# Class-by-class layout of the filtered spectrum, two tiles' statistics on swapped engines, and a new written-out order

## The chip, the core and the metric

The kernel runs on one NeuronCore of a Trainium2 chip. Five engines work side by side: TensorE (PE) multiplies matrices and writes to PSUM; VectorE (DVE) and ScalarE (ACT) read PSUM and SBUF; GpSimd (POOL) works on SBUF; SyncE (SP) starts most of the DMAs. The metric is the device time of one execution in microseconds, the median of several runs.

## What is computed

The input x has 2048 rows of 640 numbers. Each row is normalized (mean and variance over its 640 numbers). The result is the sum of x and two branches on the normalized rows: a filter in the two-dimensional Fourier domain, and a gated product of three matrices.

```python
def _A_ref(x, w_r, w_i):
    B, S, D = x.shape                                   # 1, 2048, 640
    X = jnp.fft.rfft2(x.astype(jnp.float32), axes=(-2, -1))
    X = X * (w_r + 1j * w_i)                            # (2048, 321)
    return jnp.fft.irfft2(X, s=(S, D), axes=(-2, -1)).astype(jnp.bfloat16)

def _B_ref(x, w_gate, w_up, w_down):                    # 640x1536, 640x1536, 1536x640
    g = jnp.einsum("bsd,df->bsf", x, w_gate)
    u = jnp.einsum("bsd,df->bsf", x, w_up)
    return jnp.einsum("bsf,fd->bsd", g * u, w_down)

x = A_x
xn = _layernorm(x, axis=-1)
return x + _A_ref(xn, A_w_r, A_w_i) + _B_ref(xn, B_w_gate, B_w_up, B_w_down)
```

## The kernel before

The 2048 rows are 16 tiles of 128 (tile b holds rows 16p + b on partition p). The program is a list of tasks, each with an engine, its reads and writes, and PSUM banks. The order of the tasks on every engine and the bank of each are written out by hand in the table `_PLAN` (task number, engine, bank); the semaphore waits follow from it. So an engine takes its tasks strictly in the order of the table, SP's DMAs included. Names below are the task names in the code; a number after an underscore is a tile, a chunk or a frequency group.

**Start.** 42 full matmuls on constants (`warm`) run on PE until the first tile is there; `nwarm` is their number. For each tile the statistics are made either on DVE (`bn`, two halves, then `ag`) or on ACT (`sm` for the mean, `sq` for the sum of squares); the set `aset` says which tiles are on ACT. Then `sd` (square root, ACT), `rs` (reciprocal, DVE) and `mul` (normalize in place, DVE). Tiles 0 to 3 are transposed on PE (`T0_b`, five matmuls, copied out by `eT0_b`), the others by DMA (`xt`). Tile loads are `ld_x`.

**Gate and up.** `GU_f_b_w` multiplies block f of 128 gate or up columns (w) by a chunk of rows that begins with tile b, `eG` copies it to SBUF, and `H_f_b` multiplies gate and up on DVE. This is L973 for small chunks and L951 for chunks of 512 rows.

**Fourier branch, forward.** `S1` to `S5` on DVE and `R` on PE (L905) split the 640 columns by five and two and transform along part of the rows. `D_t_w` (L1034) transforms columns, `eD` copies the result, and `C_t` (L1053) finishes the rows: 321 frequencies for each of 128 combinations, in PSUM. The 321 frequencies come as four classes of 64 (two halves of 32, the second half mirrored) and one class of 65 (every fifth frequency).

**Filter.** `WM_t` on DVE multiplies the result by w_r and w_i, with four instructions for the four classes (L1070, one for each of the two weights and the two halves) and one for the fifth class (L1073). For two t at a time, `SM_t` (L1086, L1087) combines them to real and imaginary parts in the buffer L, and `JA`, `JB` (fifth class: `JC`, `JD`, on POOL) write the parts again with real and imaginary exchanged, so that L holds, for each frequency group q, 640 columns. The weight `ld_w` loads come in pieces.

**Fourier branch, inverse.** `IA_q` (L1116) has five small matmuls, one for each class, whose stationary operand is 128 columns of L and whose moving operand is a table of 64 columns; `eIA` copies to Z2. When all of Z2 is there, `I_a` (L1144) transforms the columns back with the table g, `V1` to `V5` on DVE join the classes to 640 columns, and `IV` (L1233) adds the last step into the PSUM bank of the output.

**Output.** `ACC_a_h` (L1221) multiplies H by w_down for tile a and half h, in three pieces of 5, 4 and 3 matmuls; `IV` ends the group; `FINA` (ACT) and `FIN` (DVE) add x again (loaded once more by `ld_xr`), and `st_out` stores. Blocks of w_down (`ld_wd`) take the place of the inverse row table (`ld_ti`) as it is used up.

In the layout before, the four classes lie interleaved in L, so four of the five stationary operands of an IA are read with a step of 4 elements:

```python
yl = v_l[:, lr, o_ + 128 + k:o_ + 640:4] if k < 4 else v_l[:, lr, o_:o_ + 128]
```

Of the kernel before, what the change touches and what calls it, by code (L numbers as in the profile page):

```python
# [255 lines left out]
def _build_tables():  # L256
    t = {}
# [7 lines left out]
    for tt in range(16):  # L265
        for g in range(_G):
            q = tt * _G + g
# [36 lines left out]
    for o in range(2):  # L304
        own = (l_ % 2 == o).astype(np.float64)
        fd[64 * o:64 * o + 64, 512:577] = e.real * own[None, :]
        fd[64 * o:64 * o + 64, 578:641] = (e.imag * own[None, :])[:, 1:64]
        gd[63:128, 512 + 64 * o:576 + 64 * o] = w.real * own[:, None]
        gd[0:63, 512 + 64 * o:576 + 64 * o] = -(w.imag * own[:, None])[1:64]
# [59 lines left out]
_LP = 321  # L369
_YS = 1090  # L370
# [30 lines left out]
def _d_act(n):  # L401
# [4 lines left out]
    (12, 1, -1), (19, 2, -1), (10, 0, 1), (0, 3, -1), (11, 4, -1), (13, 4, -1), (18, 2, -1), (20, 2, -1), (28, 2, -1),  # L406
    (27, 2, -1), (170, 1, -1), (14, 4, -1), (8, 3, -1), (21, 1, -1), (22, 2, -1), (29, 2, -1), (23, 2, -1), (30, 1, -1),
    (31, 2, -1), (32, 2, -1), (24, 0, 3), (25, 2, -1), (26, 2, -1), (9, 0, 7), (33, 0, 1), (34, 2, -1), (35, 2, -1),
    (181, 0, 0), (182, 2, -1), (36, 1, -1), (37, 1, -1), (15, 4, -1), (43, 1, -1), (38, 1, -1), (169, 4, -1), (179, 0, 6),
    (180, 2, -1), (39, 2, -1), (40, 2, -1), (183, 2, -1), (44, 1, -1), (45, 1, -1), (46, 2, -1), (47, 2, -1), (189, 0, 1),  # L410
    (191, 0, 0), (190, 1, -1), (192, 1, -1), (193, 2, -1), (172, 4, -1), (186, 0, 6), (171, 4, -1), (112, 2, -1), (187, 1, -1),
    (41, 0, 2), (42, 1, -1), (184, 0, 7), (185, 1, -1), (16, 4, -1), (54, 2, -1), (113, 2, -1), (48, 0, 6), (49, 1, -1),
    (62, 1, -1), (194, 0, 5), (196, 0, 3), (197, 1, -1), (195, 1, -1), (188, 2, -1), (198, 2, -1), (50, 2, -1), (51, 2, -1),
    (53, 2, -1), (114, 2, -1), (55, 2, -1), (52, 2, -1), (63, 1, -1), (206, 0, 2), (207, 1, -1), (64, 1, -1), (204, 0, 7),
    (205, 1, -1), (115, 2, -1), (173, 4, -1), (209, 0, 6), (174, 4, -1), (65, 1, -1), (210, 1, -1), (66, 1, -1), (67, 2, -1),
    (56, 1, -1), (57, 2, -1), (116, 2, -1), (199, 0, 3), (200, 1, -1), (70, 2, -1), (201, 0, 2), (202, 1, -1), (203, 2, -1),
    (58, 2, -1), (208, 2, -1), (17, 4, -1), (121, 2, -1), (72, 1, -1), (1, 4, -1), (211, 0, 7), (175, 4, -1), (212, 1, -1),
    (176, 4, -1), (177, 4, -1), (73, 1, -1), (117, 0, 2), (118, 1, -1), (119, 0, 5), (74, 1, -1), (213, 2, -1), (122, 2, -1),
    (68, 2, -1), (123, 2, -1), (75, 1, -1), (76, 1, -1), (77, 2, -1), (216, 0, 1), (217, 1, -1), (214, 0, 0), (215, 1, -1),
    (218, 2, -1), (221, 0, 2), (222, 1, -1), (78, 2, -1), (124, 2, -1), (219, 0, 3), (220, 1, -1), (223, 2, -1), (80, 2, -1),  # L420
    (224, 0, 4), (120, 1, -1), (225, 1, -1), (82, 1, -1), (60, 2, -1), (226, 0, 2), (227, 1, -1), (229, 0, 6), (230, 1, -1),
    (83, 1, -1), (84, 1, -1), (178, 4, -1), (231, 0, 5), (125, 2, -1), (128, 0, 6), (126, 0, 3), (129, 1, -1), (232, 1, -1),
    (228, 2, -1), (130, 2, -1), (233, 2, -1), (131, 2, -1), (59, 4, -1), (71, 4, -1), (2, 4, -1), (236, 0, 0), (237, 1, -1),
    (61, 4, -1), (85, 1, -1), (234, 0, 2), (127, 1, -1), (86, 1, -1), (235, 1, -1), (238, 2, -1), (132, 2, -1), (92, 1, -1),
    (241, 0, 6), (242, 1, -1), (239, 0, 7), (240, 1, -1), (93, 1, -1), (243, 2, -1), (133, 2, -1), (87, 2, -1), (246, 0, 4),
    (244, 0, 1), (245, 1, -1), (94, 1, -1), (247, 1, -1), (248, 2, -1), (134, 2, -1), (69, 4, -1), (249, 0, 6), (250, 1, -1),
    (95, 1, -1), (96, 1, -1), (97, 2, -1), (251, 0, 2), (252, 1, -1), (90, 2, -1), (253, 2, -1), (88, 2, -1), (98, 2, -1),
    (100, 2, -1), (254, 0, 7), (255, 1, -1), (256, 0, 3), (257, 1, -1), (438, 4, -1), (433, 4, -1), (259, 0, 4), (260, 1, -1),
    (258, 2, -1), (137, 0, 5), (139, 0, 0), (437, 4, -1), (435, 4, -1), (441, 4, -1), (472, 4, -1), (101, 4, -1), (91, 4, -1),
    (434, 4, -1), (470, 4, -1), (3, 4, -1), (135, 0, 2), (136, 1, -1), (143, 2, -1), (138, 1, -1), (102, 1, -1), (261, 0, 7),  # L430
    (262, 1, -1), (79, 4, -1), (89, 4, -1), (141, 0, 3), (269, 0, 2), (263, 2, -1), (142, 1, -1), (140, 1, -1), (266, 0, 5),
    (267, 1, -1), (144, 2, -1), (270, 1, -1), (264, 0, 4), (265, 1, -1), (268, 2, -1), (145, 2, -1), (271, 0, 5), (274, 0, 1),
    (103, 1, -1), (104, 1, -1), (272, 1, -1), (273, 2, -1), (81, 4, -1), (442, 4, -1), (466, 4, -1), (146, 2, -1), (105, 1, -1),
    (106, 1, -1), (275, 1, -1), (279, 0, 4), (280, 1, -1), (276, 0, 0), (277, 1, -1), (278, 2, -1), (107, 2, -1), (147, 2, -1),
    (110, 2, -1), (108, 2, -1), (468, 4, -1), (469, 4, -1), (281, 0, 6), (282, 1, -1), (286, 0, 7), (287, 1, -1), (283, 2, -1),
    (284, 0, 3), (152, 0, 4), (148, 0, 6), (153, 1, -1), (99, 4, -1), (431, 4, -1), (440, 4, -1), (432, 4, -1), (4, 4, -1),
    (683, 4, -1), (109, 4, -1), (111, 4, -1), (473, 4, -1), (156, 2, -1), (429, 4, -1), (439, 4, -1), (467, 4, -1), (471, 4, -1),
    (149, 1, -1), (285, 1, -1), (288, 2, -1), (157, 2, -1), (150, 0, 0), (289, 0, 2), (151, 1, -1), (154, 0, 4), (291, 0, 6),
    (296, 0, 0), (290, 1, -1), (292, 1, -1), (155, 1, -1), (293, 2, -1), (158, 2, -1), (301, 0, 2), (299, 0, 6), (300, 1, -1),
    (294, 0, 4), (295, 1, -1), (304, 0, 7), (306, 0, 6), (6, 4, -1), (297, 1, -1), (298, 2, -1), (159, 2, -1), (160, 2, -1),  # L440
    (305, 1, -1), (307, 1, -1), (309, 0, 0), (310, 1, -1), (302, 1, -1), (303, 2, -1), (311, 0, 7), (312, 2, -1), (308, 2, -1),
    (163, 0, 5), (164, 1, -1), (167, 0, 1), (161, 0, 3), (162, 1, -1), (168, 2, -1), (314, 0, 0), (315, 2, -1), (313, 2, -1),
    (165, 0, 4), (316, 0, 6), (317, 2, -1), (166, 1, -1), (446, 0, 2), (447, 1, -1), (448, 2, -1), (474, 0, 0), (443, 0, 4),
# [78 lines left out]
def _build(nc, A_x, A_w_r, A_w_i, B_w_gate, B_w_up, B_w_down, out, opts=None):  # L522
# [3 lines left out]
    with es:  # L526
# [46 lines left out]
        o_end = cur[0]  # L573
        cur[0] = o_r
        b_a = alloc("A", 4 * 648)
        b_pr = alloc("PR", 8 * 321)
        b_l = alloc("L", 2 * 2624)
        b_w3 = alloc("W3", 2 * _WQ * 321)
        o_end = max(o_end, cur[0])
# [14 lines left out]
        def V(name):  # L594
            off, sz = lay[name]
            return arena[:, off: off + sz]
# [748 lines left out]
```

## Time and profile before

| | |
|---|---|
| median of 3 runs (lowest, highest) | 196.58 us (196.56, 196.6) |
| the profiled execution: its time, its span | 196.57 us, 194.9 us |
| granted TensorE clock | 1.00 |
| busy: PE, DVE, ACT, POOL | 190.9, 176.7, 136.4, 12.2 us |
| DVE in the stage 68.3 to 127.2 us | 55.96 of 58.90 us |
| gate and up, 512 rows (L951) | 440 matmuls, 101.9 us busy |
| down (L1221) | 396 matmuls, 57.2 us busy |
| IA (L1116) | 160 matmuls |
| WM (L1070 and L1073) | 64 x 414 ns and 16 x 432 ns |

The span runs from the first to the last instruction of the core; the rest of the execution's time lies around it. In a row of the groups the columns are: line, engine, operation, operands (out<-in) with their shapes, count, then busy time and the mean of one instruction in ns, and last the idle time of the engine just before them with what ended it. Matmuls overlap each other, so the mean of one is longer than the distance from one to the next; the chain gives the time that they take on the path. A piece of the chain gives its start, its length, the engine, the line and the number of instructions.

### The profile page before, as it was taken

The numbers are of one execution on the slowest core, as the hardware profiler recorded it, in microseconds if no ns is written. First come the engines' busy times: TensorE is split into PE (matmuls) and PEld (weight loads), VectorE is DVE, ScalarE is ACT, GpSimd is POOL, SyncE is SP. The second block draws the span as 40 slices with busy tenths as digits, with TensorE's granted clock in tenths as the row PEclk, the third lists the DMA queues.
The fourth block names the chain that finished last, engine by engine and source line by source line (L and its number), as shares of the span: only waits on it lengthen the run. The fifth ranks groups of instructions, "written<-read, shape, count | busy, mean of one in ns | idle before, by whom it ended". The sixth has DMA issues, their size and how long they took to land.

```text
span 194.9 us, 4074 instructions
## 1 busy us (share of the span) xinstructions
PE 190.9 (98%) x1568; PEld 120.5 (62%) x1568; DVE 176.7 (91%) x369; ACT 136.4 (70%) x275; POOL 12.2 (6%) x22
## 2 busy tenths in 40 slices
PE   8899999999999999999999999999999999999995
PEld 8797454454454565555655555557777777777774
DVE  3899999999999999999989999987999999999713
ACT  3899999999884679989999999667305523253130
POOL 1000000000000000331031221120000000000000
DMA  5999974016869921366465510005001543135412
GB/s 173 324 370 324 214 98 111 0 37 105 155 130 222 258 68 27 96 145 193 118 153 135 153 36 31 3 0 170 4 0 53 144 143 104 40 95 172 134 68 67
DMA packets 29666, 23.73 MB, mean 122 GB/s; under 512 B 10448, under 2 KB 27600, under 8 KB 29520
## 3 DMA queue, kind: packets, MB, share of 16 engines
q1 hardware_dynamic: 28848, 23.08, 46.5%
q10 hardware_dynamic: 800, 0.41, 0.7%
q8 instruction: 12, 0.20, 0.5%
q14 instruction: 6, 0.05, 0.1%
HBM read 18.89 MB, written 2.62 MB: 110 GB/s over the span
## 4 chain that ended last, share of the span: by engine, by line
PE 95%; DVE 2%; DMA 1%; ACT 1%; issue 0%
PE ps L951 48%; PE ps L1221 27%; PE ps L973 5%; PE ps L1116 3%; PE ps L1034 2%; PE ps L1053 2%; PE ps L905 2%; PE ps L1144 2%; PE ps L1233 2%; DMA arena<-in_A_x_dram 1%; DVE arena L754 1%; PE ps L814 1%; ACT arena L681 1%; DVE arena L682 0%; DVE arena L761 0%
## 5 line engine op out<-in xcount | busy, mean ns | idle before, releaser
L681 ACT ACTIVATE arena<-ps 128x512 bf16<-128x512 f32 (+5 forms) x211 | 111.3, 582 | 48.8 <-PE ps L1233 13.8
L951 PE MATMUL ps<-arena 128*128 128x512 bf16 x440 | 101.9, 379 | 0.0
L951 PEld LDWEIGHTS ps<-arena 128*128 128x128 bf16 x440 | 40.9, 98 | 43.1 <-ACT arena L681 0.9
L1221 PE MATMUL ps<-arena 128*128 128x320 bf16 (+2 forms) x396 | 57.2, 295 | 0.0
L1221 PEld LDWEIGHTS ps<-arena 128*128 128x128 bf16 x396 | 37.6, 98 | 13.2
L1070 DVE TENSOR_TENSOR arena<-ps,arena 128x256 bf16<-128x256 f32 x64 | 22.6, 414 | 1.5 <-PE ps L1053 1.3
L991 DVE TENSOR_TENSOR arena<-arena 128x512 bf16<-128x512 bf16 x44 | 18.7, 426 | 0.6 <-ACT arena L681 0.2
L1260 DVE TENSOR_TENSOR arena<-arena 128x640 bf16<-128x640 bf16 x15 | 7.0, 486 | 5.4 <-ACT arena L681 5.4
L682 DVE CAST arena<-ps 128x512 bf16<-128x512 f32 (+4 forms) x16 | 10.1, 639 | 1.5 <-PE ps L973 0.4
L745 ACT ACTIVATE arena<-arena 128x640 bf16<-128x640 bf16 x12 | 10.2, 849 | 0.1
L682 POOL COPY arena<-arena 64x252 bf16<-64x252 bf16 x8 | 4.1, 510 | 92.8 <-DVE arena L1087 92.5
L973 PE MATMUL ps<-arena 128*128 128x128 bf16 (+1 forms) x120 | 9.5, 237 | 0.3 <-DVE arena L682 0.3
L1116 PEld LDWEIGHTS ps<-arena 128*128 128x128 bf16 x160 | 7.9, 116 | 3.0
L736 ACT ACTIVATE arena<-arena 128x640 bf16<-128x640 bf16 x12 | 9.0, 753 | 0.2
L973 PEld LDWEIGHTS ps<-arena 128*128 128x128 bf16 x120 | 8.4, 98 | 1.1 <-issue 0.4
L1100 POOL TENSOR_SCALAR arena<-arena 64x252 bf16<-64x252 bf16 x8 | 7.5, 943 | 22.9 <-DVE arena L1087 22.6
L1116 PE MATMUL ps<-arena 128*128 128x64 bf16 x160 | 8.3, 198 | 0.0
L1233 PE MATMUL ps<-arena 128*128 128x320 bf16 (+2 forms) x33 | 8.3, 295 | 0.0
L1034 PEld LDWEIGHTS ps<-arena 128*128 128x128 bf16 x160 | 6.4, 98 | 2.7 <-issue 0.5
L857 DVE TENSOR_TENSOR arena<-arena 128x768 f32<-128x768 bf16 (+1 forms) x10 | 7.9, 789 | 0.0
L1073 DVE TENSOR_TENSOR arena<-ps,arena 128x260 bf16<-128x260 f32 x16 | 6.9, 432 | 0.0
L1034 PE MATMUL ps<-arena 128*128 128x64 bf16 (+1 forms) x160 | 6.9, 193 | 0.0
(61 smaller groups left out, 184.3 us busy)
## 6 DMA issues: line engine op xcount, KB each, us to landing
arena<-in_A_x_dram SPq DMA_DIRECT2D x19, 160.0 KB, 2.6
arena<-in_A_w_i_dram SPq DMA_DIRECT2D x30, 80.2 KB, 2.3
arena<-in_A_w_r_dram SPq DMA_DIRECT2D x30, 80.2 KB, 2.3
out_dram<-arena SPq DMA_DIRECT2D x15, 160.0 KB, 1.9
arena<-in_B_w_gate_dram SPq DMA_DIRECT2D x4, 320.0 KB, 6.5
arena<-in_A_x_dram SPq DMA_DIRECT2D x1, 1280.0 KB, 10.8
arena<-c_tf SPq DMA_DIRECT2D x4, 256.0 KB, 4.6
arena<-c_ti SPq DMA_DIRECT2D x2, 512.0 KB, 5.0
```

The source lines that it names most:

```text
L681: return c.e.activation(dst, src, _ACTF.Copy)
L682: return c.e.tensor_copy(dst, src)
L736: return c.e.activation(v_jk, v_x[:, b, :], _ACTF.Copy, scale=1.0 / _D, accum_out=v_m32[:, b:b + 1])
L745: return c.e.activation(v_jk, v_x[:, b, :], _ACTF.Square, scale=-1.0, bias=v_m32[:, b:b + 1], accum_out=v_ss[:, b:b + 1])
L951: ins = c.e.matmul(ps[:, bk, :], v_gw[:, w, j, ft, :], v_xt[:, j, rows], start=(j == 0), stop=(j == 4))
L973: ins = c.e.matmul(ps[:, bk, i * n:(i + 1) * n], v_gw[:, w, j, ft0 + i, :], v_xt[:, j, rows], start=(j == 0), stop=(j == 4))
L991: return c.e.tensor_tensor(v_ht[:, ft0, rows], gb[:, 0, :], gb[:, 1, :], _OP.mult)
L1034: ins = c.e.matmul(ps[:, bk + i, k * 64:k * 64 + n], v_uq[:, k, t + i, :], v_fd[:, k * 128 + w * n: k * 128 + w * n + n], start=True, stop ...
L1070: c.e.tensor_tensor(dst, xh, wv, _OP.mult)
L1116: ins = c.e.matmul(ps[:, bk, 64 * k:64 * k + 64], yl, v_ti[:, q, 0, :], start=True, stop=True)
L1221: ins = c.e.matmul(ps[:, bk, 0:sl3.stop - sl3.start], v_ht[:, ft, a * 128:(a + 1) * 128], v_wd[:, ft, sl3], start=(ft == _FT_ORDER[0]), st ...
L1233: return c.e.matmul(ps[:, bank_of(own), 0:sl3.stop - sl3.start], v_sm[:, 2, :], v_v[:, a, sl3], start=False, stop=True)
```

## The change

Each of the four classes now has a block of its own in L (64 columns, then the 64 exchanged ones), and the fifth class has one of 65 + 63. The product buffer PR has five blocks of 66 columns (`_LB`) for each group, so WM writes packed runs of 32, and reads the weights with a step of 10 elements in its innermost loop. SM takes 20 blocks of 66 columns at once; a new memset `pad` on POOL zeroes the two columns behind each block once. The fifth class now has its real part first, and the table g changes its rows to match. IA reads five packed blocks. ACT takes the statistics of tile 1 and DVE those of tile 2, where it was the other way round; `warm` has 43 matmuls for 42. The table `_PLAN` is a new one: places and banks of nearly all tasks differ, though mostly by a few places. The core of the diff, without the table:

```diff
-        gd[63:128, 512 + 64 * o:576 + 64 * o] = w.real * own[:, None]
-        gd[0:63, 512 + 64 * o:576 + 64 * o] = -(w.imag * own[:, None])[1:64]
+        gd[0:65, 512 + 64 * o:576 + 64 * o] = w.real * own[:, None]
+        gd[65:128, 512 + 64 * o:576 + 64 * o] = -(w.imag * own[:, None])[1:64]
...
-        b_pr = alloc("PR", 8 * 321)
-        b_l = alloc("L", 2 * 2624)
+        b_pr = alloc("PR", 8 * 5 * _LB)
+        b_l = alloc("L", 2 * 2560)
...
-        v_pr = V("PR").rearrange("p (w g n) -> p w g n", w=2, g=4)
-        v_l = V("L").rearrange("p (r n) -> p r n", r=2)
+        v_pr = V("PR").rearrange("p (w g b c) -> p w g b c", w=2, g=4, b=5)
+        v_l = V("L").rearrange("p (r g b c) -> p r g b c", r=2, g=4, b=5)
...
-        nwarm = opts.get("nwarm", 42)
+        nwarm = opts.get("nwarm", 43)
...
-        aset = set(opts.get("act_set", (2, 3))) | set(range(opts.get("act_stats", 6), 16))
+        aset = set(opts.get("act_set", (1, 3))) | set(range(opts.get("act_stats", 6), 16))
...
-                        xh = ps[:, bk:bk + 2, 0:256].rearrange("p g (k h m) -> p h g m k", k=4, h=2)[:, h]
-                        wv = wt[:, w, :, 0:320].rearrange("p g (m k) -> p g m k", k=10)
-                        wv = wv[:, :, :, 1:5] if h == 0 else wv[:, :, :, 9:5:-1]
-                        dst = v_pr[:, w, 2 * pb:2 * pb + 2, 65:321].rearrange("p g (h m k) -> p h g m k", h=2, k=4)[:, h]
+                        xh = ps[:, bk:bk + 2, 0:256].rearrange("p g (k h m) -> p h g k m", k=4, h=2)[:, h]
+                        wv = wt[:, w, :, 0:320].rearrange("p g (m k) -> p g k m", k=10)
+                        wv = wv[:, :, 1:5] if h == 0 else wv[:, :, 9:5:-1]
+                        dst = v_pr[:, w, 2 * pb:2 * pb + 2, 1:5, 32 * h:32 * h + 32]
...
+            if t == 0:
+                def em_pad(c):
+                    return c.e.memset(v_pr[:].rearrange("p w g b c -> p (w g b) c")[:, :, 64:_LB], 0.0)
+                T("pad", "pool", 300.0, em_pad, writes=[(b_pr, None)], prio=pq - 0.002)
...
-                pa_, pb_ = v_pr[:, 0], v_pr[:, 1]
-                l_ = v_l[:, lr, 63:2623].rearrange("p (g n) -> p g n", g=4)[:, :, 0:321]
+                pa_, pb_ = (v_pr[:, w].rearrange("p g b c -> p (g b) c") for w in range(2))
+                l_ = v_l[:, lr].rearrange("p g b c -> p (g b) c")[:, :, 0:_LB]
...
-                src = l0[:, :, 1:64] if five else l0[:, :, 65:321]
-                dst = l1[:, :, 0:63] if five else l0[:, :, 321:577]
+                src = v_l[:, lr, :, 0, 1:64] if five else v_l[:, lr, :, 1:5, 0:64]
+                dst = v_l[:, lr, :, 0, 65:128] if five else v_l[:, lr, :, 1:5, 64:128]
...
-                        yl = v_l[:, lr, o_ + 128 + k:o_ + 640:4] if k < 4 else v_l[:, lr, o_:o_ + 128]
+                        yl = v_l[:, lr, q % 4, (k + 1) % 5]
```

What the new table does to the places that matter below:

- PE at the start: before T0_0, fill, T0_1, then four GU; after T0_0, fill, one GU, T0_1, three GU.
- DVE at the start: before both bn of tiles 0 and 1, then rs_0 and mul0; after rs_0 and mul0 directly behind ag0, and bn2 between mul1 and the copy of T0_1.
- SP: x3 ahead of x2; ld_fd at place 40 (was 18); ld_wd4 behind ld_wd6 and four ld_xr.
- Middle: DVE takes JB_7, JB_9 and JA_13, ACT takes JA_9 and JA_15; some copies change between them. The IA that first read the last two SM (IA_27, IA_30) stand ahead of one GU that was ahead of them before.
- End of the middle: GU_11_12_0 is behind the last IA, and three more H (blocks 4 to 6 of the last chunk) run on DVE behind the last IA.

## The prediction

> **What bounds the kernel now.** I read the busy table, the chain that ended last, that chain in order of time, the groups split by shape, and the timeline of the first ten microseconds.
>
> ```profile
> PE 190.9 (98%) x1568; PEld 120.5 (62%) x1568; DVE 176.7 (91%) x369; ACT 136.4 (70%) x275; POOL 12.2 (6%) x22
> ...
> PE 95%; DVE 2%; DMA 1%; ACT 1%; issue 0%
> ```
>
> A busy PE need not be a bound one, but the second row says that the end is reached by walking back along PE for 95% of the span. The chain in order of time shows where PE takes over and where it lets go, and among its pieces two kinds of small matmul, both 64 columns wide (a few 65):
>
> ```profile
> 7.31 2.95 PE ps L973 x50
> ...
> 69.05 0.89 PE ps L1034 x30
> ...
> 81.64 0.67 PE ps L1116 x20
> ...
> 192.60 0.29 DVE arena L1242
> ```
>
> From 7.31 to 192.60 the chain leaves PE once for about 1 us (near 65); summing its gaps I find well under 1 us of waiting. So the time is made of four parts: 7.31 us until the first gate/up product, 185.3 us of PE work, 2.3 us of tail (last add, last store, end), and 1.67 us outside the span (196.57 of the profiled run minus 194.9). Only fewer PE nanoseconds, an earlier first product, or a new hole in PE can move the result. The median of the runs is 196.58, so sums against the profiled run carry over as they are.
>
> DVE is the second to watch. The stage table gives it 55.96 busy of the 58.90 us between 68.3 and 127.2, the stage of WM and SM: 2.9 us are free there and no more.
>
> **Part 1, contiguous weights of the inverse column products (IA).** The groups by shape:
>
> ```profile
> L1116 PEld LDWEIGHTS ps<-arena 128*128 128x128 bf16 x160 | 7.9, 116 | 3.0
> ...
> L1034 PEld LDWEIGHTS ps<-arena 128*128 128x128 bf16 x160 | 6.4, 98 | 2.7 <-issue 0.5 <-ACT arena L681 0.2
> ```
>
> Same matmul form, same count, 116 against 98 ns per weight load. IA (L1116) reads four of its five weight tiles with a step of 4 elements, D (L1034) reads all of them packed. On the chain IA has 2.8% of 194.9 us, so 5.46 us or 34.1 ns each; D has 2.4%, 4.68 us or 29.2 ns each. The x20 and x30 pieces above say the same (33.5 and 29.7). With 64 columns the weight load, not the streaming, sets the pace, so packing IA's weights should bring it to D's pace: 160 x 4.9 ns = **0.8 us less**, all on the path, since IA stands between other PE work. Against this stands the Trainium skill, "TensorE: Matmul & The Clock Gate", section "Weight-path perf modes": its fast weight load reads four chunks of 32 columns "packed or strided", with a column step up to 1,024 elements, and it names no price for the step. By that rule a step of 4 costs nothing, the 0.8 us would be 0, and the sum below would end at 196.8. I take the rows: 116 and 98 ns are of one shape in one run.
>
> **Part 2, what pays for it: the writes of WM, SM and J.** WM now walks the weights (w_r, w_i) with the class outside and 32 elements inside, so its second operand jumps 10 elements (20 bytes) at each element; before it read four neighbours and then jumped. Rows:
>
> ```profile
> L1070 DVE TENSOR_TENSOR arena<-ps,arena 128x256 bf16<-128x256 f32 x64 | 22.6, 414 | 1.5 <-PE ps L1053 1.3
> ...
> L1073 DVE TENSOR_TENSOR arena<-ps,arena 128x260 bf16<-128x260 f32 x16 | 6.9, 432 | 0.0
> ```
>
> L1073 already reads the same weights with a step of 5 (10 bytes), and its 260 elements take 18 ns more than 256: no cost of the step. The Trainium skill, "SBUF — State Buffer", note on SBUF "cachelines", says otherwise for the new step: lines are 16 bytes, at least two reads should fall in one, and bf16 strides for free up to 8 elements. Ten is past that; every read opens a new line. No row here has such a step. By the row WM stays at 414 ns, cost 0. By the rule it pays; bounds: 0 below (nothing in the new pattern is shorter, the element count is the same), and above one more cycle per element. A 320-wide and a 256-wide cast differ by 60 ns (486 and 426), so 0.94 ns per element and 240 ns per instruction, 64 x 240 = 15.4 us. I take the row, L1073 being the same operand at half the step, and keep the rule as a rival.
>
> SM goes from 1284 to 1320 elements per instruction at (824 - 426)/(1284 - 512) = 0.52 ns each (L1086 against L991, a 512-wide product): +19 ns x 16 = 0.3 us on DVE, covered by its 2.9 us. JA and JB keep 1024 elements and packed runs (64 instead of 256 long): 0, between -0.05 and +0.05 us each. JC and JD on POOL now start at an odd element on the side(s) that were even:
>
> ```profile
> L682 POOL COPY arena<-arena 64x252 bf16<-64x252 bf16 x8 | 4.1, 510 | 92.8 <-DVE arena L1087 92.5
> ...
> L1100 POOL TENSOR_SCALAR arena<-arena 64x252 bf16<-64x252 bf16 x8 | 7.5, 943 | 22.9 <-DVE arena L1087 22.6
> ```
>
> The trace has no odd start on POOL; SM on DVE had odd starts and ran at its full pace, so I take 0, bounded by -0.2 and by a doubling (+1.45 us per pair). A pair was finished 1 to 4 us ahead of the IA that reads it, so a small change hides. The new memset on POOL (80 elements; a 1-element memset takes 0.10) waits for the last S5 at about 65.5 and must be done before the first WM at 72.7. It stands alone on POOL, with JD_1 at about 78 behind it: 0, with 7 us of cover.
>
> **Part 3, the start: tile 1's statistics to ACT, tile 2's to DVE.**
>
> ```profile
> 4.18 0.21 DVE L761 BATCH_NORM_AGGREGATE arena<-arena 128x2 f32<-128x12 f32 x1
> 4.37 0.89 DVE L754 BATCH_NORM_STATS2 arena<-arena 128x6 f32<-128x320 bf16 x2
> 4.42 0.29 ACT L771 ACTIVATE arena<-arena 128x1 f32<-128x1 f32 x1 [1.34 <-DVE arena L761]
> ...
> 5.18 0.15 DVE L778 RECIPROCAL arena<-arena 128x1 f32<-128x1 f32 x1
> ...
> 5.42 0.39 DVE L795 TENSOR_SCALAR arena<-arena 128x640 bf16<-128x640 bf16 x1
> ```
>
> ACT had tile 0's deviation at 4.71, but DVE was inside tile 1's statistics until 5.26. With those gone the reciprocal runs at 4.75 at the latest, the multiply ends near 5.3 and T0_0 can start at 5.4 instead of 5.87. The warm-up of 43 (105 to 107 ns each from 0.84) ends its issue near 5.4: the extra one bridges and costs nothing more. Walking on with the same durations: T0_0 still at the slow pace, 5.4 to 5.9; its two copies on DVE; GU_0_0_1 at 6.85 (was 7.31). T0_1 is now late: on ACT, sm1 from 4.45, sq1, sd_1 take 0.86 + 0.94 + 0.29, rs_1 and mul1 end at 7.3, T0_1 runs behind GU_0_0_1 at 7.4 and ends at 7.85. Its DVE copy stands behind bn2 (two at 0.41 us from mul1 on) and starts at 8.0, so GU_0_1 starts at 8.5, with PE idle from 8.25. T0_2 waits for mul2, behind two GU copies, H_0_0 and two reciprocals, until 10.2 to 10.3. T0_3, which has the same PE work ahead of it in both orders, comes at about 11.1 where it was at 10.94. So the half microsecond won at T0_0 is spent: **+0.15 us**, between -0.2 and +0.4. Loads: x2 is now queued behind x3, one slot (0.47 us); tile 2 is wanted at 7.2, tile 3 at 6.4, and in the run before they were read from 5.89 and 7.76 on without a wait. The gate weights of GU_0_0_0 (issued at 2.67, 4.9 us to landing, so 7.6) are wanted at 7.7: just in time.
>
> **Part 4, the new order.** Most PE neighbours only change places. Three changes bear on the end. (a) DVE gets about 1.1 us more before the last SM (JB_7, JB_9, JA_13, one D copy and two IA copies come, JA_9, one GU copy and one H go): with SM's 0.3 it leaves 1.5 of the 2.9 us. (b) IA_27 and IA_30 move ahead of one GU (1.08 us), and PE reaches them 0.5 to 0.7 us sooner by Part 1. Before, POOL finished 2.0 us ahead of the first IA of each of these groups (122.6 against 124.4, 128.6 against 130.7). Minus 1.08, minus 0.6, minus up to 0.7 of later DVE leaves about -0.4 to +0.3: I put **+0.1 us** for a short wait, 0 to 0.8. (c) The last IA is now followed by GU_11_12_0, so its copies have 1.08 us where they had ACC's 0.68 before I_1 needs all of Z2. SP: ld_fd moves from place 18 to 40 behind a wait for mul15 (53.6), lands near 59 and is wanted at 68.9; the transposes of tiles 4 to 7 land by 32 for 35; ld_wd4 goes behind ld_wd6 and four x loads (five slots of 0.46), lands near 135 and is wanted by the third piece of ACC_1_0 near 136.8. All hidden. Tail: the last product and its store stay the same, 0.
>
> **Sum.** 196.57 - 0.8 + 0.15 + 0.1 = 196.02; I say **196.0**, own range 195.5 to 196.3.
>
> **The rivals.** *A, the step of 10 costs DVE (15%, slower).* Place: L1070's successors, 64 instructions, in the stage with 1.5 us of DVE slack. PE is held once 64 x price exceeds that; the gain of 0.55 is gone at (1.5 + 0.55)/64 = 32 ns each, and 0.2% slower than before at 38 ns. IA's weight loads lose 18% to a step; the same on 240 ns is 44 ns, 2.8 us, and PE is held 1.3 us: 197.3. With one more cycle per element, 15.4 - 1.5 = 13.9 us: 210. For it: the rule, and no row with such a step. Against: L1073, and the old PSUM operand that jumped 64 elements at each read at full pace.
>
> *B, the order gives the gain back (25%).* The holes of Parts 3 and 4 at their upper ends: 196.57 - 0.8 + 0.4 + 0.5 = 196.7, down to 196.2. For it: PE's releases in the middle often come within 0.1 us of use. Against: those margins were held before without holes.
>
> *C, packing does not speed IA (5%).* By the fast-weight rule: 196.8. Against it, D's row.
>
> **Chances.** The forecast has 55%. About 0.2% (0.4 us) is what a measurement can tell from no change. Faster: 0.47 from the forecast, 0.10 from B; within: 0.08, 0.10, and 0.03 from C; slower: 0.15 from A, 0.05 from B, 0.02 from C. Range 195.4 to 197.4: it takes in the start's gain below, A's first price above, and leaves out A's heavy end.
>
> **What would show it.** IA's weight loads at 98 ns and its pieces of 20 in 0.58 us; WM still at 414 ns, SM at 843; first GU near 6.9, a PE hole near 8.3, T0_3 near 11.1; the last DVE add at about 192.0. I am wrong if WM's rows grow, if POOL's rows double and IA waits for them, or if IA stays at 34 ns.

## The result, and the profile after

The changed kernel takes **209.66 us** (median of 5 runs, 209.61 to 210.0) against 196.59 for the kernel before: a ratio of 1.067, 95% interval 1.0655 to 1.0686. It is 13.07 us slower, where 0.6 less was forecast. The profiled span went from 194.9 to 208.3 us at a granted clock of 1.00 in both. Line numbers below are those of the changed kernel: WM's class products are L1071 (L1070 before), its fifth class L1074 (L1073), SM L1091 and L1092 (L1086, L1087), IA L1118 (L1116).

The busy table of the page after, and the first line of the chain that ended last:

```profile
PE 192.4 (92%) x1552; PEld 118.2 (57%) x1569; DVE 190.0 (91%) x371; ACT 136.7 (66%) x273; POOL 12.8 (6%) x23
...
PE 41%; DVE 36%; ACT 11%; DMA 5%; SPq 3%; issue 3%; DVEq 0%
```

PE's busy time is about what it was, DVE has 13.3 us more, and the walk back from the end now goes along DVE for 36% of the span where it was 2%. (The trace after lacks 17 of the 440 records of the 512-row gate and up products, so PE's sum and count are a little low.) The groups of the page after, split by shape, in the order busy us, mean ns of one, idle time before:

```profile
L1071 DVE TENSOR_TENSOR arena<-ps,arena 128x256 bf16<-128x256 f32 x64 | 34.9, 609 | 0.5 <-PE ps L1054 0.3
L1074 DVE TENSOR_TENSOR arena<-ps,arena 128x260 bf16<-128x260 f32 x16 | 7.0, 437 | 0.0
L1091 DVE TENSOR_TENSOR arena<-arena 64x1320 bf16<-64x1320 bf16 x8 | 6.7, 842 | 0.3
L1118 PEld LDWEIGHTS ps<-arena 128*128 128x128 bf16 x160 | 6.2, 98 | 7.7 <-DVE arena L1074 3.4 <-issue 1.7 <-DVE arena L1103 1.1
```

One row carries the result. Each of the 64 class products takes 609 ns instead of 414: the same 256 elements, the same operands, but each weight is now read 10 elements (20 bytes) behind the last. From start to start two of them are 523 ns apart (median) where they were 332, and 64 x 191 ns = 12.2 us. SM has the 842 ns that were forecast, and IA's weight loads fell from 116 to 98 ns as forecast, but the loads now wait 7.7 us where they waited 3.0. The waits of the trace after say for what (us in total, times, longest):

```profile
PEld ps L952 <- DVE arena L1074: 4.1, 5, 1.2
PEld ps L1035 <- DVE arena L1074: 3.8, 4, 1.6
PE ps L1118 <- DVE arena L1074: 3.4, 5, 1.2
...
PE ps L1054 <- DVE arena L1092: 1.7, 3, 0.7
```

L1074 is the last instruction of a WM task; its end frees the two PSUM banks of C, and whatever PE wants next has to wait for a bank. So gate and up (L952), D (L1035) and IA (L1118) stand behind DVE; in the kernel before nothing on PE waited for this instruction. The stage from the first D to the first I (inverse columns), as windows (length, then busy us of PE, PEld, DVE, ACT, POOL), before and after:

```profile
68.90:132.10 63.20, 63.16 (x579) 35.22 (x578) 59.84 (x136) 57.10 (x103) 11.63 (x16) 1.00 0.34 89
```

```profile
68.90:144.80 75.90, 64.64 (x565) 32.95 (x574) 73.30 (x138) 56.37 (x100) 12.12 (x16) 1.00 0.37 89
```

Nearly the whole loss is in this stage, 63.2 to 75.9 us: PE was full in it and now has holes of 11 us, and DVE is full. Of the 13.4 us that the span grew, 0.4 come ahead of it (in this run the first D starts at 69.31) and 0.7 behind it, where the new order has put one piece of ACC (0.7 us) that stood ahead of the first I.

### The profile page after: what moved, and what is told of

Its sections match the earlier page's. It is cut to its first block, busy times and chain, and to the rows that moved or that the text cites. A ratio compares the mean times of both kernels' runs of the same rounds, so it can differ in the third digit from the quotient of the medians.

```text
span 208.3 us, 4064 instructions
## 1 busy us (share of the span) xinstructions
PE 192.4 (92%) x1552; PEld 118.2 (57%) x1569; DVE 190.0 (91%) x371; ACT 136.7 (66%) x273; POOL 12.8 (6%) x23
## 4 chain that ended last, share of the span: by engine, by line
PE 41%; DVE 36%; ACT 11%; DMA 5%; SPq 3%; issue 3%; DVEq 0%
PE ps L1223 25%; DVE arena L1071 16%; PE ps L952 10%; ACT arena L682 6%; DMA arena<-in_A_x_dram 5%; DVE arena L992 4%; SPq L676 3%; DVE arena L1092 3%; DVE arena L1091 3%; DVE arena L1074 3%; ACT arena L746 2%; ACT arena L737 2%; DVE arena L683 2%; PE ps L1146 2%; PE ps L1235 2%
## 5 line engine op out<-in xcount | busy, mean ns | idle before, releaser
L682 ACT ACTIVATE arena<-ps 128x512 bf16<-128x512 f32 (+7 forms) x210 | 111.8, 578 | 62.3 <-PE ps L1235 20.3
L952 PE MATMUL ps<-arena 128*128 128x512 bf16 x423 | 100.2, 379 | 3.3 <-DVE arena L1074 1.9
L952 PEld LDWEIGHTS ps<-arena 128*128 128x128 bf16 x440 | 40.5, 98 | 47.6 <-DVE arena L1074 4.1
L1223 PE MATMUL ps<-arena 128*128 128x320 bf16 (+2 forms) x396 | 56.8, 295 | 0.0
L1223 PEld LDWEIGHTS ps<-arena 128*128 128x128 bf16 x396 | 37.7, 98 | 13.4
L1071 DVE TENSOR_TENSOR arena<-ps,arena 128x256 bf16<-128x256 f32 x64 | 34.9, 609 | 0.5 <-PE ps L1054 0.3
L683 DVE CAST arena<-ps 128x320 bf16<-128x320 f32 (+4 forms) x17 | 10.3, 621 | 1.9 <-PE ps L1118 0.6
L1118 PE MATMUL ps<-arena 128*128 128x64 bf16 x160 | 7.3, 193 | 4.1 <-DVE arena L1074 3.4
L1118 PEld LDWEIGHTS ps<-arena 128*128 128x128 bf16 x160 | 6.2, 98 | 7.7 <-DVE arena L1074 3.4
L1103 POOL TENSOR_SCALAR arena<-arena 64x252 bf16<-64x252 bf16 x8 | 8.1, 1009 | 28.0 <-DVE arena L1092 27.6
L1035 PEld LDWEIGHTS ps<-arena 128*128 128x128 bf16 x160 | 6.2, 98 | 5.6 <-DVE arena L1074 3.8
L974 PEld LDWEIGHTS ps<-arena 128*128 128x128 bf16 x120 | 8.4, 98 | 1.6 <-issue 0.7
L1035 PE MATMUL ps<-arena 128*128 128x64 bf16 (+1 forms) x160 | 7.0, 193 | 2.6 <-DVE arena L1074 2.6
L1054 PE MATMUL ps<-arena 128*128 128x321 bf16 x32 | 6.6, 299 | 1.8 <-DVE arena L1092 1.7
L1235 PE MATMUL ps<-arena 128*128 128x320 bf16 (+2 forms) x33 | 7.9, 295 | 0.0
L796 DVE TENSOR_SCALAR arena<-arena 128x640 bf16<-128x640 bf16 x16 | 6.9, 445 | 0.1
```

The costliest lines, as they stand in the source:

```text
L682: return c.e.activation(dst, src, _ACTF.Copy)
L683: return c.e.tensor_copy(dst, src)
L952: ins = c.e.matmul(ps[:, bk, :], v_gw[:, w, j, ft, :], v_xt[:, j, rows], start=(j == 0), stop=(j == 4))
L974: ins = c.e.matmul(ps[:, bk, i * n:(i + 1) * n], v_gw[:, w, j, ft0 + i, :], v_xt[:, j, rows], start=(j == 0), stop=(j == 4))
L1035: ins = c.e.matmul(ps[:, bk + i, k * 64:k * 64 + n], v_uq[:, k, t + i, :], v_fd[:, k * 128 + w * n: k * 128 + w * n + n], start=True, stop ...
L1071: c.e.tensor_tensor(dst, xh, wv, _OP.mult)
```

## The experiments

There are three theories of the loss. *R*: a read step of 10 elements has a price of its own on DVE, whatever stands around it. *O*: the new order, or the new layout's other parts, bring part of it, or the old order would have hidden it. *W*: the class walk is bad in another way (where it writes, for one), so that turning it round another way would cost as much.

**1. The classes inside again, the layout kept.** WM reads four neighbours as before, and so has to write with a step of 66 elements (132 bytes).

```diff
-  xh = ps[...].rearrange("p g (k h m) -> p h g k m", k=4, h=2)[:, h]
-  wv = wt[...].rearrange("p g (m k) -> p g k m", k=10)
+  xh = ps[...].rearrange("p g (k h m) -> p h g m k", k=4, h=2)[:, h]
+  wv = wt[...].rearrange("p g (m k) -> p g m k", k=10)
-  dst = v_pr[:, w, 2 * pb:2 * pb + 2, 1:5, 32 * h:32 * h + 32]
+  dst = v_pr[:, w, 2 * pb:2 * pb + 2, 1:5, 32 * h:32 * h + 32].rearrange("p g k m -> p g m k")
```

> The changed kernel, everything of it kept (packed IA, swapped statistics, new order), but WM's four class instructions walk the four neighbouring weights innermost again, as before; so it is the write to PR that now jumps (66 elements, 132 bytes) and the weight read that doesn't. Theory R (the 20-byte step of the weight read costs the time): WM's rows fall from 609 to about 414 ns, PE's holes between 73 and 142 us go, and the time is 196.59 - 0.8 (IA) + 0.23 (the start as measured, T0_3 at 11.17 for 10.94) + 0 to 0.5 = 196.0 to 196.5. Rival W (each element on a line of its own costs, read or written): WM stays near 600 ns and the time near 209. Rival O (the new order starves PE): WM may fall, the time stays above 204.

Measured: 251.49 us, ratio 1.279 (1.274 to 1.284). The class products by their line, min/median/max:

```profile
L1071 DVE TENSOR_TENSOR arena<-ps,arena x64: 1281/1513/1534, 73.5 to 178.6; 128x256 bf16<-128x256 f32 x64
```

The kernel got 42 us slower still. The packed read did not help, because a product with the strided write takes 1513 ns, two and a half times the 607 (median) of one with the strided read. So W was right that writing has a price, and moving the step from the read to the write is no way to have the layout. R is not tested by this run, whose write hides everything else.

**2. The kernel before with only WM's walk turned**: read step 10, and write step 4, since its layout keeps the classes interleaved. Its order, layout and IA stay.

```diff
-  xh, wv: "... g m k";  dst = v_pr[...].rearrange("p g (h m k) -> p h g m k", h=2, k=4)[:, h]
+  xh, wv: "... g k m";  dst = v_pr[...].rearrange("p g (h m k) -> p h g k m", h=2, k=4)[:, h]
```

> The kernel before, its layout and its order kept; only WM's loops are turned, so that the weights are read with a step of 10 elements and written with a step of 4. Theory R: WM rows about 607 ns; 64 x 193 ns = 12.4 us more on DVE, of which the 2.9 us of free DVE time in the stage take a part: 205 to 209. Rival O (new order): WM may be slower, but the old order hides it: below 198.

Measured: 211.15 us, ratio 1.0748 (1.0734 to 1.0762), above the 205 to 209 that R expected.

```profile
L1070 DVE TENSOR_TENSOR arena<-ps,arena x64: 723/792/840, 72.6 to 139.1; 128x256 bf16<-128x256 f32 x64
```

The old order does not hide slower products, so that part of O falls. The 792 ns are 185 more than the 607 of the changed kernel, so the read step is not alone here: the write step of 4 elements has a price too, and experiment 4 shows that it could account for all of the 792 ns. What the read step alone costs in the old order is left to experiment 9.

**3. A map of read steps.** Writes packed, the weights read with a different step in each row set.

```diff
+  st = (1, 2, 3, 4, -4, 5, 6, 7, 8, 9, 10, 12, 16, 20, 32, 40)[t]
+  if 0 < st < 5: wv = v_wr[wr][:, w, 0:256 * st]...[..., 0]          # 256 reads, step st
+  else:          wv = v_wr[wr][:, w, 0:32 * abs(st)]... "p (m s) -> p s m" [:, 0:4], both g alike
```

> The changed kernel with another weight-read step in each of the 16 WM (t = 0 to 15): 1, 2, 3, 4 (eight runs), 4 (the first operand's runs again), 5, 6, 7, 8, 9, 10, 12, 16, 20, 32, 40 elements of bf16. It multiplies by other weights than the reference's, so only the times count. Theory R in the form of 16-byte lines: 410 to 420 ns up to a step where two reads fall in one line (5 to 8), a full price for every step over 8; if a line change costs one cycle, 10 elements and more give about 650. Rival R2 (price grows smoothly with the share of reads that open a new line): already 5 and 6 lie over 414, and 10 to 40 are alike near 607 to 650. Rival R3 (a step costs nothing, what costs is PSUM read packed beside it): all near 607.

Measured: 204.59 us (one run; only the lengths of the products are read from it). Rows of the timeline on DVE, each with start, length and the number of products. WM takes the row sets in the order of the table, so the rows are of the sets 4, 5, 6, 7, 9, 8, 11, 10 and 14, and the steps are 4, 5, 6, 7, 9, 8, 12, 10 and 32:

```profile
86.82 1.41 DVE L1076 TENSOR_TENSOR arena<-ps,arena 128x256 bf16<-128x256 f32 x4
88.49 1.52 DVE L1076 TENSOR_TENSOR arena<-ps,arena 128x256 bf16<-128x256 f32 x4
...
94.20 1.74 DVE L1076 TENSOR_TENSOR arena<-ps,arena 128x256 bf16<-128x256 f32 x4
...
96.19 2.00 DVE L1076 TENSOR_TENSOR arena<-ps,arena 128x256 bf16<-128x256 f32 x4
...
103.21 2.20 DVE L1076 TENSOR_TENSOR arena<-ps,arena 128x256 bf16<-128x256 f32 x4
105.67 2.17 DVE L1076 TENSOR_TENSOR arena<-ps,arena 128x256 bf16<-128x256 f32 x4
111.87 2.15 DVE L1076 TENSOR_TENSOR arena<-ps,arena 128x256 bf16<-128x256 f32 x4
114.28 2.20 DVE L1076 TENSOR_TENSOR arena<-ps,arena 128x256 bf16<-128x256 f32 x4
...
128.75 2.07 DVE L1076 TENSOR_TENSOR arena<-ps,arena 128x256 bf16<-128x256 f32 x4
```

The lengths of one product (mean of four): 410 to 418 ns for steps 1 to 4, 442 at 5, 501 at 6, 578 at 7, 608 at 8, then nearly level: 618 at 9, 627 at 10, 605 at 12, 598 at 16, 592 at 20, 583 at 32. The 678 at 40 stay unexplained. The price rises from step 5 and is whole at step 8, which is 16 bytes, where no two reads fall in one stretch of 16. Up to 32 it is about flat after that, as a price for each 16-byte line would be: (607 - 412)/256 = 0.76 ns for each element. Of the three forms in the expectation it is the gradual one, R2. Step 10 is past the knee; R stands.

**4. The same map for writes**, the weights read packed and the fifth class left out.

```diff
+  st, j = (1, 2, 3, 4, 5, 8, 16, 32)[t // 2], 4 * pb + 2 * w + h
+  dst = 256 elements of PR with step st; the eight products of a pair of row sets interleave
```

> One look at durations. The changed kernel with packed reads of the weights as in e4_packed_read, and with the results of the class products written with a step that differs by pair of row sets: 1, 2, 3, 4, 5, 8, 16, 32 elements; the fifth-class products are left out, and the values are not the reference's. If writes are priced as reads were: 415 ns up to a step of 4, 440 at 5, 600 from 8 on. If a write to part of a line costs more, as the run with step 4 suggests (some 185 ns on top of the read's price): about 600 ns at 4 already, and 1200 or more at 16 and 32, with the rise beginning at 2 or 3.

Measured: 217.48 us (one run, read like the last one). The timeline rows for the write steps 2, 3, 4, 5, 8, 16 and 32, eight products each:

```profile
79.19 2.80 DVE L1077 TENSOR_TENSOR arena<-ps,arena 128x256 bf16<-128x256 f32 x8 [0.29 <-PE ps L1054]
86.10 3.64 DVE L1077 TENSOR_TENSOR arena<-ps,arena 128x256 bf16<-128x256 f32 x8 [0.34 <-PE ps L1054]
93.48 5.02 DVE L1077 TENSOR_TENSOR arena<-ps,arena 128x256 bf16<-128x256 f32 x8
103.08 6.05 DVE L1077 TENSOR_TENSOR arena<-ps,arena 128x256 bf16<-128x256 f32 x8
112.73 9.27 DVE L1077 TENSOR_TENSOR arena<-ps,arena 128x256 bf16<-128x256 f32 x8
125.81 8.79 DVE L1077 TENSOR_TENSOR arena<-ps,arena 128x256 bf16<-128x256 f32 x8
137.60 9.16 DVE L1077 TENSOR_TENSOR arena<-ps,arena 128x256 bf16<-128x256 f32 x8
```

One product (median of eight): 412 ns at step 1, 437 at 2 (from start to start 330 to 346, where it is 330 to 341 at step 1), 585 at 3, 827 at 4, 984 at 5, 1513 at 8, and no more beyond (1437 at 16, 1492 at 32). The second guess held in kind: the price begins at step 3 (a read is free up to step 4, a write up to 2) and levels at the same 16 bytes, at (1513 - 412)/256 = 4.3 ns for each element, nearly six times the read's. Its 600 ns at step 4 were too low. The 827 ns there, with packed reads, are not less than the 792 of experiment 2, which also read with a step of 10: the two prices do not add (the places written differ a little between the two runs).

**5. The layout, the order and the rest, without the read price.** The changed kernel, with WM's weights read from packed places:

```diff
-  wv = wt[:, w, :, 0:320].rearrange("p g (m k) -> p g k m", k=10)[:, :, 1:5 or 9:5:-1]
+  wv = v_wr[wr][:, w, 0:256].rearrange("p (g k m) -> p g k m", g=2, k=4)
```

> The changed kernel with one thing altered: the column weights of the class products are read from packed places (step 1 in place of 10), so they are the wrong weights and the values of the output change; the layout, the new order, the exchanged statistics and the packed inverse weights all stay. Theory R (the whole loss is the read step of 10 elements in the class products): each of the 64 falls from 609 to 412-417 ns and the time to 196.0-196.6 us (196.6 - 0.8 for the packed inverse weights + 0.23 for the later start + 0 to 0.5 for the order). Rival O (the new order or the class rows cost something of their own behind the products): the products fall as said, and the time stays above 198.

Measured: 197.44 us, ratio 1.0047 (1.003 to 1.0063), the products at 414 ns. So the read step is 209.66 - 197.44 = 12.2 us of the 13.07, as much as 64 x 191 ns: in this order all of it goes through to the time. But 197.44 is 0.8 us above the kernel before, and as much above the upper end of what R expected: even with free reads the change is a loss, and so the prediction had a second error.

**6. What packed inverse weights are worth.** Two pairs, one on each side of the read price: the kernel of experiment 5, and that of experiment 1, each with IA reading its weights with a step of 4 again.

```diff
-  yl = v_l[:, lr, q % 4, (k + 1) % 5]
+  fl = v_l[:, lr, q % 4].rearrange("p b c -> p (b c)")
+  yl = fl[:, 128 + k:640:4] if k < 4 else fl[:, 0:128]
```

> The same as e4_packed_read, but the inverse column products read their weights with a step of 4 elements, as in the kernel before (the weights are then the wrong ones). Nothing holds VectorE back here, so this pair shows what the packed weights are worth by themselves. By the prediction's figure, 160 loads that pace at 34 in place of 29 ns: 0.7 to 0.9 us above e4_packed_read. If the pace of TensorE is not what ends these stages: under 0.3.

> The run e1_classes_inside with one thing more: IA reads its weights with the old addresses, a step of 4 elements for four of five, so it multiplies other columns of L than the reference's. Theory: IA's weight loads go back from 98 to 116 ns and its matmuls from 29 to 34 ns, PE gets 0.8 to 0.9 us more, and the time is 0.7 to 0.9 us above e1_classes_inside. Rival (the gain is hidden, DVE or ACT bound the middle): within 0.3 us of it.

Measured: 197.68 us (197.43 to 198.21, ratio 1.0052, 1.0037 to 1.0067) beside 197.44: 0.24 more, inside the spread of the two, though IA's weight loads went from 98 to 116 ns. The other pair, 250.81 us (ratio 1.277, 1.273 to 1.281) beside 251.49, is inconclusive: DVE ends the stage there by tens of microseconds, so IA's pace cannot show. Here the step forecast for IA, 0.7 to 0.9, failed.

**7. The new order alone**: the kernel before with the new `_PLAN`, the exchanged statistics and 43 warming products.

> The kernel before, with its layout, its class products and its inverse products as they were, but with the new order, with tiles 1 and 3 in place of 2 and 3 taking their statistics on ScalarE, and with 43 warming products. By the prediction: 0.15 to 0.25 us from the later start and 0 to 0.3 from the order, so 196.7 to 197.2. Rival O (the order brings much of the loss): above 199.

Measured: 197.17 us, ratio 1.0024 (1.0014 to 1.0034), so 0.5 us slower, twice what was put on start and order together. Its first D starts at 68.92 us and that of the kernel before at 68.89, so the later T0_3 is made up again by then and costs nothing at the end. What is lost is lost later: the last SM starts at 127.33 us instead of 126.34. The DVE groups of the kernel before between 68.5 and 130.5 us,

```profile
L682 DVE COPY arena<-arena 64x1024 bf16<-64x1024 bf16 x6 | 2.7, 452 | 0.2
L1100 DVE TENSOR_SCALAR arena<-arena 64x1024 bf16<-64x1024 bf16 x5 | 2.6, 517 | 0.2
L682 DVE CAST arena<-ps 64x642 bf16<-64x642 f32 x3 | 2.5, 826 | 0.1
...
L682 DVE CAST arena<-ps 128x320 bf16<-128x320 f32 x2 | 1.0, 486 | 0.0
```

and in the new order:

```profile
L1100 DVE TENSOR_SCALAR arena<-arena 64x1024 bf16<-64x1024 bf16 x7 | 3.3, 478 | 0.2
L682 DVE CAST arena<-ps 64x642 bf16<-64x642 f32 x4 | 3.3, 826 | 0.1
L682 DVE COPY arena<-arena 64x1024 bf16<-64x1024 bf16 x5 | 2.4, 471 | 0.1
...
L682 DVE CAST arena<-ps 128x320 bf16<-128x320 f32 x4 | 1.9, 486 | 0.1
```

Two JB, one copy of D and two of IA have come, one JA has gone. Windows from the first WM to the end of the last SM, before and in the new order:

```profile
72.73:127.16 54.43, 54.39 (x484) 30.06 (x483) 51.98 (x122) 50.71 (x92) 10.33 (x14) 1.00 0.37 98
```

```profile
72.75:128.15 55.40, 54.49 (x477) 29.65 (x485) 54.20 (x126) 49.50 (x90) 10.65 (x14) 1.00 0.46 111
```

DVE has 54.20 us of work there where it had 51.98: 2.2 more, not the 1.1 that the prediction put for the same tasks (the GU copy that it took off runs ahead of the first WM). DVE's idle time went from 2.45 to 1.20 us, and no run of this case has less than 1.1 there; so 1.25 us of the work was covered, not up to 2.9, and the stretch is 1.0 us longer. In experiment 5 it holds 54.48 us of work and the time is 0.27 higher than here: that is SM's 0.3 us, which this order does not cover either.

**8. The class layout with packed reads, in the old order** (experiment 5 with the old `_PLAN`, statistics and warm-up).

> The class layout of the changed kernel, with the weights of the class products read from packed places as in e4_packed_read (the wrong weights, so other values), but in the order of the kernel before, with its statistics (tiles 2 and 3) and its 42 warming products. Theory E (in the new order VectorE ends the stage of the columns, since that order gives it one more mirror copy, one more eviction of 64x642 and two more of 128x320, and so the packed inverse weights show nothing there; in the old order TensorE ends it): 195.7 to 196.1 us, 0.5 to 0.9 below the kernel before. Rival (the packed inverse weights are worth nothing in any order): 196.5 to 197.0.

Measured: 196.36 us, ratio 0.9987 (0.998 to 0.9993): 0.2 us below the kernel before, between the two forecasts, and less than 0.2%. Even in the order where PE was thought to end the stage, 0.8 us less PE work brings 0.2. How little room DVE has beside it, WM's row shows, here of experiment 8,

```profile
L1070 DVE TENSOR_TENSOR arena<-ps,arena 128x256 bf16<-128x256 f32 x64 | 22.6, 417 | 1.1 <-PE ps L1054 1.0
```

and of experiment 5:

```profile
L1070 DVE TENSOR_TENSOR arena<-ps,arena 128x256 bf16<-128x256 f32 x64 | 22.6, 414 | 0.5 <-PE ps L1054 0.3
```

DVE sits idle before these products for only 1.5 us in the kernel before, 1.1 here, and 0.5 in the new order (0.3 of that before the very first), nearly all of it for C results. Most of its other idle time in the stage of WM is gaps of some 28 ns between instructions (some 40 of them, 1.2 us of the 2.9), and in no run did these go. In the new order the two engines end the stage together: the chain of experiment 5 goes back along DVE for 35% of the span. Here, in the old order, it still goes along PE for 92% and along DVE for 1%, so the trace does not show DVE as what swallows the gain. PE's weight loads wait 1.4 us in the stage for ACT's copies where they waited 0.9; where the rest of the 0.6 us goes stays open. The chain of experiment 8:

```profile
PE 92%; ACT 3%; DMA 2%; issue 1%; DVE 1%; SPq 0%; ACTq 0%
```

**9. The changed kernel complete, in the old order.**

> The changed kernel complete, with its class layout and its class products that read with a step of 10, but in the order of the kernel before, with its statistics (tiles 2 and 3) and its 42 warming products. Theory R (the read price goes through to the time one for one, and the new order costs its 0.5 on top): the packed read in the old order took 196.36; with 64 products that start 191 ns further apart that is 12.2 more, so 208.3 to 208.9, 0.8 to 1.3 below the changed kernel. Rival (the new order was made to hide the products' new length and gives back some of it): 210 or more.

Measured: 207.3 us, ratio 1.055 (1.0533 to 1.0568), 1 us under the lower end forecast. It adds 10.94 to experiment 8, not 12.2: of the 1.1 us that DVE still sat idle before its products 0.1 are left, as WM's row shows:

```profile
L1071 DVE TENSOR_TENSOR arena<-ps,arena 128x256 bf16<-128x256 f32 x64 | 34.9, 607 | 0.1
```

And the new order costs 209.66 - 207.3 = 2.4 us here, against 0.5 in the old layout. It is the same work moved to DVE, now without cover: from the first WM to the end of the last SM DVE is busy 64.32 us in this run and 66.70 in the changed kernel, 2.4 more, and it is idle for 1.1 and 1.2.

```profile
72.68:138.08 65.40, 56.41 (x480) 29.53 (x487) 64.32 (x122) 52.77 (x93) 10.26 (x14) 1.00 0.29 81
```

```profile
73.13:141.02 67.89, 57.07 (x479) 28.70 (x487) 66.70 (x126) 50.97 (x91) 10.58 (x14) 1.00 0.37 91
```

The layout by order, in us (beside these runs the kernel before took 196.5 to 196.65):

| | old order | new order |
|---|---|---|
| old layout | 196.6 | 197.2 |
| class layout, packed reads | 196.4 | 197.4 |
| class layout, step 10 | 207.3 | 209.7 |

**10. The gather on GpSimd, a complete version.** POOL is busy 12 us in all, so it copies each row set's weights into class order ahead of WM, in the old order. Two weight loads are in flight in place of three, and each task on POOL waits for the one before it.

```diff
+  def em_rw(c):                                   # POOL, once for each row set
+      for w in range(2):
+          for h in range(2):
+              src = wt[:, w, :, 0:320].rearrange("p g (m k) -> p g k m", k=10)[:, :, 1:5 or 9:5:-1]
+              c.e.tensor_copy(v_pk[:, pb, w, 256 * h:256 * h + 256], src)
+      c.e.tensor_copy(v_pk[:, pb, :, 512:642], wt[:, :, :, 0:321:5])
-  reads=[(b_wr[wr][0], ...)]                      # WM
+  reads=[(b_pk, ("r", pb, pb + 1))]
```

> A complete version: the class layout in the order of the kernel before, with GpSimd copying the weights of each row set from their natural places into the order of the classes (5 copies, 1284 elements a partition) ahead of the class products, which then read packed; two loads of weights in flight in place of three, and each GpSimd instruction waits for the one before it. The class products fall to 414 ns. If GpSimd takes about 2 ns an element, as in its copies of 64x252 (507 ns), a set takes 2.6 us of the 3.4 that the products of a set have, and the time is 195.8 to 196.8 us. If a strided read costs GpSimd as it costs VectorE, or its sharing with VectorE slows either, a set takes over 4 us, GpSimd ends the stage, and the time is 205 us or more.

Measured: 244.77 us, ratio 1.243 (1.240 to 1.247). Groups on POOL, and then on DVE:

```profile
L1074 POOL COPY arena<-arena 128x256 bf16<-128x256 bf16 x64 | 47.4, 783 | 34.0 <-DVE arena L1090 30.5 <-DMA arena<-in_A_w_r_dram 2.6 <-POOL arena L1119 0.2
L1076 POOL COPY arena<-arena 128x260 bf16<-128x260 bf16 x16 | 10.2, 638 | 0.0
```

```profile
L1087 DVE TENSOR_TENSOR arena<-ps,arena 128x256 bf16<-128x256 f32 x64 | 22.6, 416 | 36.9 <-PE ps L1059 36.8
L1108 DVE TENSOR_TENSOR arena<-arena 64x1320 bf16<-64x1320 bf16 x8 | 8.8, 1104 | 0.1
...
L1090 DVE TENSOR_TENSOR arena<-ps,arena 128x260 bf16<-128x260 f32 x16 | 6.7, 422 | 0.0
```

A copy with a read step of 10 takes POOL 783 ns for 256 elements, one with step 5 takes 638 for 260; before, 252 packed elements took 510. A set is 4 x 783 + 638 = 3.8 us, and POOL has 68 us of work for a stage that took 63 before, too much even without a wait. WM is at 416 ns as it should be, and then waits 37 us for C. PE, ahead of C, waits 32 us at IA for the JC and JD that POOL makes behind its copies, and the copies wait 30.5 us for WM to free a buffer. So the expectation's second case came, though at 244.77. SM and H are slower beside the copies (1046 and 1104 for 842 and 840 ns, and 518 for 426 over the 44 of its form); in experiment 1, at much the same granted clock, SM took its 842 and 840. How much of the 48 us is POOL's own work, how much the disturbance and how much the circle of waits around two buffers, this one run does not tell.

No run that computes the whole result is faster than the kernel before. Experiment 8 says what there is to win in the old order: 0.2 us, with a gather that is free, and none was found.

## Why the prediction failed, step by step

- **Part 2, the step of 10: failed, and decided the result.** "By the row WM stays at 414 ns, cost 0." The row was L1073, step 5, whose 18 ns over L1070 were read as "no cost of the step". Four elements more cost some 4 ns at 0.94 each, and with packed weights, in experiment 10, this instruction takes 422 ns for 432: so 10 of the 18 were the step's, the foot of the rise that experiment 3 shows (442 for 412 at step 5). The nearest row stood on the near side of a knee. The Trainium skill, "SBUF — State Buffer", note on SBUF "cachelines", had said 16-byte lines and two reads in each; the map agrees with both, and the price is whole where a second read no longer fits. It differs in where reads stop being free: after 4 elements here, not 8. Measured, 195 ns for each product; the upper bound was 240.
- **Rival A came true, at its heavy end.** It gave 13.9 us (15.4 less 1.5 of slack) and 210; the runs give 12.2 and 209.66. Its mechanism and its place were right. Its slack was right for the old order only, where 12.2 became 10.9; in the new one all 12.2 came. That its 210 is so near is in part luck: the price was put too high, and the order too low. Its first price, 44 ns, was taken over from TensorE's weight loads, and no run connects the two.
- **Part 1, packed weights of IA: the mechanism right, the term mis-sized.** 98 ns for each load came true, and from one matmul to the next it is 29 ns for 34, so TensorE works 0.8 us less and rival C falls. But the time moves by 0.24 (experiment 6) or 0.2 us (experiment 8). "All on the path" was the failing step. A chain that goes back along PE for 95% of the span says that PE was last nearly everywhere, not by how much: by 1.5 us over DVE in this stage. In the new order DVE takes the path; in the old one the trace does not say what swallows the gain.
- **Part 3, the start: nearly right in sum, without effect.** T0_3 starts at 11.17 us for 10.94 (0.23, where 0.15 was forecast). The hole that was put near 8.3 is not there; PE waits 0.58 us ahead of 6.5 and 0.29 ahead of T0_1 at 7.5. In experiment 7 the first D does not start later for it.
- **Part 4, the order: 0.1 forecast, 0.5 measured alone**, and 2.4 where DVE ends the stage. The work that it moves to DVE was put at 1.1 us and is 2.2 to 2.4. The 2.9 us to cover it were the stage's length less the busy sum, gaps between instructions included; what could be used was 1.25 (experiment 7), near the 1.5 of WM's row.
- **SM +19 ns and JC, JD at 0: right in length.** 842 ns for 843; JC and JD take 507 and 1009 ns, and 512 and 1013 in experiment 7 with the old layout, 505 and 938 in experiment 8 with the new one: their odd starts cost nothing, and JD's 66 ns come with the order. That SM's 0.3 us would be covered is not so in the new order (0.27 more in experiment 5 than in 7); for the old one no run separates it.
- **What would have been the sum** along the runs of the new order: 196.6, + 0.5 for the order, + 0.3 for the layout with free reads, + 12.2 for the read step, makes 209.6. By the old order the parts are others (-0.2, + 10.9, + 2.4): the prices depend on what else fills DVE, so none of them is a property of its part alone.

## What to carry to other kernels

Before a layout is turned to please one engine, price the step that it hands to another: in this case, on DVE, a read step of up to 4 bf16 elements was free, from 8 on it cost about 0.76 ns for each element, and a write step of 8 or more 4.3 ns; a row at a smaller step says nothing of a larger one when there is a knee between them, and a forecast has to keep the upper bound in its range. Slack was what the engine waited for someone else in the rows of its own instructions, not the window less its busy time. And where two engines end a stage within a microsecond or two of each other, a saving on the one can be worth far less than its size (0.2 of 0.8 us here), while work added to the other costs all but what it had been waiting (10.9 of 12.2 us, and all of it where nothing was left).

## What the runs showed of the hardware that was not expected

- From a step of 8 on, a strided write costs VectorE nearly six times what a strided read does (4.3 and 0.76 ns for each element), and it starts to cost at step 3 (585 ns for 256 elements), not 5. A step of 2 is free by the distance of starts.
- The two prices do not add: a write step of 4 takes 827 ns with packed reads (experiment 4), and 792 with a read step of 10 (experiment 2).
- A copy with a step of 10 on GpSimd takes 3.1 ns for each element, and SM's sum on VectorE beside it takes 1104 ns instead of 840.
- The granted TensorE clock was 0.93 in experiment 1, 0.94 in its partner of experiment 6, 0.92 in experiment 10 and 0.98 in experiment 4, the four longest runs, in which PE waits most; it was 1.00 in all the others. No run here tells why.
